# Laying the gate and silu tiles at the end of SBUF, and normalising row tile 1 before the statistics of row tile 2

## The chip, the cores and the metric

The kernel runs on one core of a Trainium2 chip. The metric is the device time of one execution in microseconds (us), as a median over several runs. A profile records one execution, and its span runs from the first to the last recorded instruction.

## The reference

The computation takes 2048 rows `x` of width 640, normalises them, and runs an attention block and a feed-forward block on the same normalised rows. The feed-forward result, passed through silu, gates the attention result, and `x` is added back.

```python
def reference(A_x, A_k_cache, A_v_cache, A_wq, A_wo, B_x, B_w_gate, B_w_up, B_w_down):
    def _A_ref(x, k_cache, v_cache, wq, wo):
        ...                                    # 32 heads of width 192, the last 512 keys alone
        scores = jnp.einsum("bhqd,bhkd->bhqk", q, k) * (Dh ** -0.5)
        p = _softmax(scores, axis=-1)
        o = jnp.einsum("bhqk,bhkd->bhqd", p, v)
        return (lambda x, *d: x.transpose(*d))(o, 0, 2, 1, 3).reshape(B, Sq, Hq * Dh) @ wo
    def _B_ref(x, w_gate, w_up, w_down):       # 640 -> 1536 -> 640
        g = _silu(x @ w_gate)
        u = x @ w_up
        return (g * u) @ w_down
    x = A_x
    xn = _layernorm(x, axis=-1)
    s = _A_ref(xn, A_k_cache, A_v_cache, A_wq, A_wo)
    g = _silu(_B_ref(xn, B_w_gate, B_w_up, B_w_down))
    return x + s * g
```

## The kernel before

Every engine executes its instructions in the order in which the program writes them; the order is written out by hand, and no scheduler changes it. There are three stages. The first normalises the rows and computes the feed-forward block. It leaves the transposed normalised rows in SBUF (`xnT`) and the gates in DRAM (`g_d`, 160 KB for each of 16 row tiles, stored on the SP queue by line 467 from the tiles `g_t`). The second computes the attention, two heads (a pair) at a time, in phases whose order is a table of tokens. The third multiplies by `wo`, applies the gates and stores the output.

**The opening.** The rows come in 16 row tiles of 128 rows; four of them make a block of 512. The first block is handled row tile by row tile. For row tile t, VectorE (DVE) takes two `bn_stats` over half rows (line 336) and a `bn_aggr` (line 339); ScalarE (ACT) takes the square root (line 368); DVE inverts it (line 377) and writes the normalised rows `xn` (line 379); TensorE (PE) transposes them with five matmuls against the identity (line 565); ACT copies the result into `xnT` in two parts (line 573). `ln_stats(t, between)` calls `between` after its first `bn_stats`. `ready(t)` issues the transposes and the copies, with the square root of row tile t + 1 between the two copies for t of 1 and 2.

```python
ln_stats(0)
ln_sqrt(0)
ln_stats(1, lambda: ln_apply(0, (slice(0, 2 * P), slice(2 * P, D))))
ready(0)
ln_sqrt(1)
...
for t in range(4):
    ...
    for k, (f, s, cs) in enumerate(order):
        if k == len(order) * 7 // 10 and t < 3:
            ...                                # the lines that the diff changes
            ready(t + 1)
        hidden_mm(first[f][s][:, rows], s, f, rows, cs)
```

`hidden_mm` (line 394) is one matmul, or five of them, of the gate or up projection, into six PSUM banks. So the transposes of row tile t + 1 stand in PE's order after 21 of the 30 matmuls of row tile t; for t = 0 the nine that follow read the late part of the up weights, `wu_sb`. The rows and the first weights are loaded on the SP and ACT queues in the order x tile 0, x tile 1, first weights, x tile 2, x tile 3, the other weights.

**The first stage's tiles.** Its pools are stacked from the end of SBUF downwards, in the order in which they are opened: `ffw` (weights, one scratch tile), `lnw` and `lnx` (statistics, `x_t` and `xn`), `ffh` (two hidden tiles `hT`), `ffa` (three `sg` tiles, which hold silu of the gate projection, and two `g_t` tiles). When the stage ends, all are closed, and the pools of the later stages take their bytes: `out_first` (operands of the third stage) from the end of SBUF downwards, then `m_f`, the two value tiles `V_p`, and `att_p` (nine `p_t` tiles for the exponentials of the scores). The first writer of a new tile waits for the last users of what lay there; in `att_p` the first tile waits for all users of the whole pool's bytes.

**The turn into attention.** The last gates are computed by ACT (line 464) and stored (line 467). The first phase then runs: scores (line 786, into two `sc` buffers of PSUM), exponentials on ACT (`p_t`, line 790), the queries in three forms (lines 717 and 729, added up by DVE in line 722 or by ACT, GpSimd and DVE with `m_f` in lines 747, 764, 767, 771 and 777), and probabilities times values (line 825). SP loads the values and transposes the keys of the next pair by DMA (`KT`, line 219). DVE sums those keys (line 227) and centres them (lines 236 and 238). In DVE's order the three key sums stand after the third line 722, and ahead of the first line 767, which PE needs before the next line 729 into the same bank.

Of the kernel before, what the change touches and what calls it, by code (L numbers as in the profile page):

```python
# [15 lines left out]
def kernel(  # L16
# [241 lines left out]
    a_q, b_w = {}, {}  # L258

    with ExitStack() as fctx:  # L260
        ffw = fctx.enter_context(tc.tile_pool(name="ffw", bufs=1, side="right"))
        lnw = fctx.enter_context(tc.tile_pool(name="lnw", bufs=4, side="right"))
        lnx = fctx.enter_context(tc.tile_pool(name="lnx", bufs=8, side="right"))
        ffh = fctx.enter_context(tc.tile_pool(name="ffh", bufs=2, side="right"))
        ffa = fctx.enter_context(tc.tile_pool(name="ffa", bufs=3, side="right"))

        zero_t = q_all[:, 0, :]
        nc.vector.memset(zero_t, 0.0)
# [61 lines left out]
        def ln_stats(t, between=None):  # L330
            b, ti = divmod(t, 4)
            if ti == 0:
                ln[b] = [lnw.tile([P, 4, 2], f32, name="mv"), lnw.tile([P, 4], f32, name="rstd")]
            stats = lnw.tile([P, ng, nc.vector.BN_STATS_DIM], f32, name="stats")
            for g in range(ng):
                nc.vector.bn_stats(stats[:, g, :], x_t[t][:, g * (D // ng) : (g + 1) * (D // ng)])
                if g == 0 and between:
                    between()
            nc.vector.bn_aggr(ln[b][0][:, ti, :], stats[:])
# [32 lines left out]
        def ln_apply(t, parts=(slice(0, D),)):  # L372
            b, ti = divmod(t, 4)
            mv, rstd = ln[b]
            xns[t] = lnx.tile([P, D], bf, name="xn", bufs=4)
            if b == 0:
                nc.vector.reciprocal(rstd[:, t : t + 1], rstd[:, t : t + 1])
            for cols in parts:
                nc.vector.tensor_scalar(
                    xns[t][:, cols], x_t[t][:, cols], mv[:, ti, 0:1] if b < 2 else mv[:, ti : ti + 1],  # L380
                    rstd[:, ti : ti + 1], op0=ALU.subtract if b < 2 else ALU.add, op1=ALU.mult,
                )
# [8 lines left out]
        def hidden_mm(out, s, f, qc, cs=range(NC)):  # L391
            w_sb = (wg_sb, wu_sb)[s]
            for c in cs:
                nc.tensor.matmul(  # L394
                    out, w_sb[:, c, f * P : (f + 1) * P], xnT[:, c, qc],
                    start=(c == 0), stop=(c == NC - 1),
                )

        def hidden_gate(b, f, g, u):
            sg = ffa.tile([P, 512], bf, name="sg")  # L400
            nc.scalar.activation(sg[:], g, ACT.Silu)  # L401
            nc.vector.tensor_tensor(hTs[b][:, f, :], u, sg[:], ALU.mult)  # L402
# [157 lines left out]
        def ready(t):  # L560

            xn, rows = xns.pop(t), slice(t * P, (t + 1) * P)
            for tp, cs in zip(tps, PARTS):
                for k, c in enumerate(range(cs.start, cs.stop)):
                    nc.tensor.transpose(tp[:, k, :], xn[:, c * P : (c + 1) * P], ident[:])
            for tp, cs in zip(tps, PARTS):
                part = tp[:, 0 : cs.stop - cs.start, :]
                if cs.stop == NC and 1 <= t < 3:
                    ln_sqrt(t + 1)
                if t == 3 and cs.stop == NC:  # L570
                    nc.vector.tensor_copy(out=xnT[:, cs, rows], in_=part)
                else:
                    nc.scalar.copy(xnT[:, cs, rows], part)
# [7 lines left out]
        for t in range(4):  # L581
            rows = slice(t * P, (t + 1) * P)

            order = [(*fs, [c]) for c in range(NC) for fs in banks]
            if t == 0:
                order = order[:12] + [
                    (f, s, [c]) for s in range(2) for c in range(2, NC) for f in range(3)
                ]
            elif t == 3:
                order = [(*fs, range(NC)) for fs in banks]  # L590
            for k, (f, s, cs) in enumerate(order):
                if k == len(order) * 7 // 10 and t < 3:
                    if t < 2:
                        ln_stats(t + 2, lambda: ln_apply(t + 1))
                    else:
                        ln_apply(t + 1)
                    ready(t + 1)
                    if t == 2:
                        nc.scalar.activation(act_t[:], one_t[:], ACT.Silu)
                hidden_mm(first[f][s][:, rows], s, f, rows, cs)  # L600
                if t == 3 and s == 1:
                    hidden_gate(0, f, *first[f])
# [573 lines left out]
    for s in range(PHASES_N):  # L1176
        table = FIRST if s < 4 else LAST if s >= PHASES_N - 4 else PHASES
        for x in table[s % 4].split():
            name = x.lstrip("+<")
# [55 lines left out]
```

## Time and profile before

| | |
|---|---|
| Median of three runs | 873.0 us (871.72 to 877.42) |
| The profiled execution: its time | 872.65 us |
| Its span | 870.8 us |
| PE busy | 860.6 us (99% of the span) |
| DVE, ACT, GpSimd busy | 588.4, 450.4, 165.9 us |
| Clock granted to TensorE | 1.0 of full speed |

A busy share is an average over the span. The profile's view of waits says who waited for whom, its timeline gives each engine's instructions in order, its chain of waits follows the end of the program back to what released each step, and a view of stretches gives busy times between two points of the span. Start times are in us from the start of the span.

### The profile page before, as it was taken

Reading aid. Unit: us, or ns where it says so; the run is one execution under the profiler, and the core shown is the slowest. Engines: PE = TensorE matmul, PEld = TensorE weight load, DVE = VectorE, ACT = ScalarE, POOL = GpSimd, SP = SyncE. Lnnn points to the kernel's source line nnn. Section 1 sums busy time; section 2 is a strip of 40 time slices with the busy share of each in tenths; the row PEclk is TensorE's granted clock in tenths of the full one; section 3 lists DMA queues with packets and bytes.
Section 4 is the critical chain, followed back from the end, with each engine's and each line's share of the span. In section 5 each row is a group of like instructions: output and inputs, shape, how many; then the busy total and the mean of one; then the engine's idle time right before and its main releaser. Section 6 shows DMA issues by size and latency. Waiting matters only on the chain.

```text
span 870.8 us, 22711 instructions
## 1 busy us (share of the span) xinstructions
PE 860.6 (99%) x9619; PEld 571.6 (66%) x9635; DVE 588.4 (68%) x1023; ACT 450.4 (52%) x634; POOL 165.9 (19%) x247
## 2 busy tenths in 40 slices
PE   8999999999999999999999999999999999999998
PEld 5455555567666666666666666666676777777776
DVE  6643666777777777777777777777755786655564
ACT  4264434567777677667667667667668400000000
POOL 0000000013224333333333333333331000000000
PEclk9999999999999999999999999999999999999999
DMA  9424423457789988988988967788898986655410
GB/s 298 95 46 112 84 72 84 96 99 135 179 162 161 186 179 176 229 178 180 232 173 191 224 147 175 173 184 163 191 223 197 268 283 223 211 178 174 176 54 16
DMA packets 264678, 143.87 MB, mean 165 GB/s; under 512 B 173696, under 2 KB 260480, under 8 KB 264576
## 3 DMA queue, kind: packets, MB, share of 16 engines
q1 hardware_dynamic: 263792, 141.77, 70.1%
q8 instruction: 75, 1.23, 0.6%
q10 hardware_dynamic: 784, 0.65, 0.2%
q14 instruction: 27, 0.22, 0.1%
HBM read 76.58 MB, written 30.41 MB: 123 GB/s over the span
## 4 chain that ended last, share of the span: by engine, by line
PE 96%; DMA 2%; ACT 1%; issue 0%; DVE 0%; ACTq 0%; POOL 0%; POOLq 0%; SPq 0%
PE acc L943 21%; PE sc L786 19%; PE mm L825 14%; PE mm L729 12%; PE sc L394 11%; PE sc L729 7%; PE mm L455 5%; PE sc L825 5%; PE mm L717 1%; PE sc L522 1%; DMA x_t<-in_A_x_dram 1%; ACT p_t L790 0%; PE gu L394 0%; DMA o_d<-OT_b 0%; DMA g_d<-g_t 0%
## 5 line engine op out<-in xcount | busy, mean ns | idle before, releaser
L790 ACT ACTIVATE p_t<-sc 128x1024 bf16<-128x1024 f32 x256 | 258.3, 1023 | 88.9 <-PE sc L786 86.1
L786 PE MATMUL sc<-q_all,khat 64*128 64x512 bf16 x1536 | 206.5, 376 | 2.3 <-ACT p_t L790 1.7
L825 PEld LDWEIGHTS <-p_t 64*128 64x128 bf16 x4096 | 179.7, 94 | 36.8 <-issue 0.6
L825 PE MATMUL mm<-V_p,p_t 64*128 64x193 bf16 x3008 | 157.3, 243 | 0.5 <-ACT O_b L854 0.3
L729 PEld LDWEIGHTS <-w_all 64*128 64x128 f16 (+1 forms) x1540 | 86.0, 94 | 71.4 <-issue 0.6
L786 PEld LDWEIGHTS <-khat 64*128 64x128 bf16 x1536 | 82.6, 94 | 58.4 <-issue 8.2
L771 POOL TENSOR_TENSOR m_f<-m_f 128x1024 f32<-128x1024 f32 x44 | 105.3, 2394 | 41.1 <-DVE r L843 15.0
L729 PE MATMUL mm<-xc,w_all 64*128 64x512 f16 x890 | 112.0, 376 | 0.0
L767 DVE TENSOR_TENSOR q_all<-mm,m_f 128x1024 bf16<-128x1024 f32 x44 | 53.9, 1224 | 56.2 <-ACT m_f L764 56.1
L943 PE MATMUL acc<-b_w,a_q 128*128 128x320 bf16 (+1 forms) x576 | 81.8, 299 | 0.0
L848 DVE TENSOR_TENSOR O_b<-mm,r 128x384 bf16<-128x384 f32 x151 | 78.3, 553 | 3.1
L993 ACT COPY xc<-acc 128x320 f32<-128x320 f32 x8 | 3.4, 426 | 135.7 <-PE acc L943 135.7
L802 POOL MEMSET turn_t<- 128x1 f32 x128 | 12.7, 99 | 314.8 <-PE mm L825 239.6
L943 PEld LDWEIGHTS <-a_q 128*128 128x128 bf16 x576 | 56.3, 98 | 22.0 <-issue 0.2
L402 DVE TENSOR_TENSOR hT<-sc,sg 128x512 bf16<-128x512 f32 x46 | 31.7, 691 | 55.2 <-ACT sg L401 55.2
L943 PEld LDWEIGHTS <-q_all 128*128 128x128 f16 x552 | 52.7, 98 | 19.1
L401 ACT ACTIVATE sg<-sc 128x512 bf16<-128x512 f32 x46 | 27.3, 596 | 67.7 <-PE sc L394 65.9
L777 DVE TENSOR_TENSOR q_all<-mm,m_f 128x1024 bf16<-128x1024 f32 x44 | 53.7, 1219 | 11.6 <-POOL m_f L771 7.8
L394 PE MATMUL sc<-xnT,wg_sb 128*128 128x512 bf16 (+1 forms) x247 | 59.5, 353 | 0.8
L394 PE MATMUL sc<-xnT,wu_sb 128*128 128x512 bf16 (+1 forms) x260 | 60.3, 354 | 0.0
L943 PE MATMUL acc<-b_w,q_all 128*128 128x320 f16 (+2 forms) x432 | 58.1, 292 | 0.0
L825 PE MATMUL sc<-V_p,p_t 64*128 64x193 bf16 x1088 | 53.7, 243 | 0.3 <-POOL turn_t L802 0.3
(125 smaller groups left out, 958.8 us busy)
## 6 DMA issues: line engine op xcount, KB each, us to landing
o_d<-OT_b SPq DMA_DIRECT2D x64, 384.0 KB, 4.1
a_q<-o_d SPq DMA_DIRECT2D x32, 768.0 KB, 6.3
wq_rows<-in_A_wq_dram SPq DMA_DIRECT2D x16, 480.0 KB, 4.6
wq_rows<-in_A_wq_dram SPq DMA_DIRECT2D x30, 240.0 KB, 5.5
K_p<-in_A_k_cache_dram SPq DMA_DIRECT2D x32, 192.0 KB, 3.4
V_p<-in_A_v_cache_dram SPq DMA_DIRECT2D x32, 192.0 KB, 4.2
b_w<-in_A_wo_dram SPq DMA_DIRECT2D x12, 480.0 KB, 4.4
g_d<-g_t SPq DMA_DIRECT2D x16, 160.0 KB, 1.8
```

The lines of the kernel that those rows point to most:

```text
L394: nc.tensor.matmul(out, w_sb[:, c, f * P : (f + 1) * P], xnT[:, c, qc], start=(c == 0), stop=(c == NC - 1),)
L402: nc.vector.tensor_tensor(hTs[b][:, f, :], u, sg[:], ALU.mult)
L455: nc.tensor.matmul(ps, left[:, c, :], D_OF[m][:, c, :], start=(first and c == 0), stop=(c == KD - 1), skip_group_check=True,)
L729: nc.tensor.matmul(ps[:, h, :], ws[h][r, c, :], xs[h][r, c, :], start=(first and c == 0), stop=(c == NC - 1), skip_group_check=True,)
L767: nc.vector.tensor_tensor(to[:, 1:3, :], st["ps"][:, :, :], m_f[:, 5:3:-1, :], ALU.add)
L771: nc.gpsimd.tensor_tensor(SIDE, diag, SIDE, ALU.subtract)
L777: nc.vector.tensor_tensor(to[:, 0:4:3, :], st["ps"][:, :, :], SIDE, ALU.add)
L786: nc.tensor.matmul(sc[:, h, :], khat[r, j, ks], q_of(i, j)[r, :], start=(j == 0), stop=(j == 2))
L790: nc.scalar.activation(p_t[:, :, :], sc[:, :, :], ACT.Exp, scale=scale)
L825: m = nc.tensor.matmul(acc[:, k, h * 256 : h * 256 + Dh + 1], Ps[i][kc][r, h, qt * P : (qt + 1) * P], V_of[i // NB % 2][r, kc, h, 0 : Dh + 1],
L848: nc.vector.tensor_tensor(O_b[:, qt, :, :], a_k[:, :, 0:Dh], r[:, k, :, :].to_broadcast([P, 2, Dh]), ALU.mult,)
L943: nc.tensor.matmul(ps[:, 0:w], at[:, c, :], b_w[m][:, c, k * w : (k + 1) * w], start=(first and c == 0), stop=(c == KH - 1), skip_group_ch ...
```

## The change

The pool `ffa` is opened first of the five, not last. So the `sg` and `g_t` tiles take the last 5632 bytes of each SBUF partition, and every other tile of the first stage's pools moves 5632 bytes down; nothing else moves. In the opening, for t = 0 alone, the normalisation of row tile 1 is written ahead of both `bn_stats` of row tile 2, where before it stood between them. Lines after 593 have numbers higher by 3 in the changed kernel.

```diff
     with ExitStack() as fctx:
+        ffa = fctx.enter_context(tc.tile_pool(name="ffa", bufs=3, side="right"))
         ffw = fctx.enter_context(tc.tile_pool(name="ffw", bufs=1, side="right"))
         lnw = fctx.enter_context(tc.tile_pool(name="lnw", bufs=4, side="right"))
         lnx = fctx.enter_context(tc.tile_pool(name="lnx", bufs=8, side="right"))
         ffh = fctx.enter_context(tc.tile_pool(name="ffh", bufs=2, side="right"))
-        ffa = fctx.enter_context(tc.tile_pool(name="ffa", bufs=3, side="right"))
...
                 if k == len(order) * 7 // 10 and t < 3:
-                    if t < 2:
+                    if t == 0:
+                        ln_apply(t + 1)
+                        ln_stats(t + 2)
+                    elif t == 1:
                         ln_stats(t + 2, lambda: ln_apply(t + 1))
                     else:
                         ln_apply(t + 1)
```

The bytes of an SBUF partition that matter, before and after:

| tile | before | after | tiles of the later stages over the old bytes |
|---|---|---|---|
| `sg`, `g_t` | 134368 to 140000 | 223712 to 229344 | `p_t` (133856 to 152288) |
| `hT` (two) | 140000 to 164576 | 134368 to 158944 | `p_t`, `V_p`, `m_f` |
| `x_t` | 164576 to 174816 | 158944 to 169184 | `m_f` (158688 to 170976), `out_first` |
| `xn` | 174816 to 179936 | 169184 to 174304 | `out_first` (170976 to 229344) |
| weights, `s_sum` | 180448 to 229344 | 174816 to 223712 | `out_first` |

## The prediction

> **What bounds the kernel now.** First the page.
>
> ```profile
> span 870.8 us, 22711 instructions
> PE 860.6 (99%) x9619; PEld 571.6 (66%) x9635; DVE 588.4 (68%) x1023; ACT 450.4 (52%) x634; POOL 165.9 (19%) x247
> ```
>
> PE is the bound, and is without work for 870.8 - 860.6 = 10.2 us, 1.2% of the span. Nothing here removes PE work, so a gain is a part of these 10.2 us. The view of PE's waits names two places that the diff touches (total, times, longest):
>
> ```profile
> PE sc L786 <- ACT p_t L790: 1.7, 1, 1.7
> PE tp L565 <- DVE xn L379: 1.6, 2, 0.9
> ```
>
> The first lies at the turn into attention. The chain of waits of that stretch (start, length, what):
>
> ```profile
> 165.54 3.17 DMA g_d<-g_t
> 168.72 0.02 issue
> 168.74 0.04 ACTq L790
> 168.78 0.05 issue
> 168.82 1.03 ACT p_t L790
> 169.85 0.04 issue
> 169.90 0.82 PE sc L786 x6
> ```
>
> The first exponential waits until the last gate store has landed, since `p_t` lies where `g_t` lay. ACT's timeline has it idle for 1.79 us before 168.82; PE, with both `sc` buffers full, waits 1.72 us for the exponential's end.
>
> The second place is the opening, in the timeline (start, length, engine, line, what, idle before):
>
> ```profile
> 6.33 0.21 DVE L339 BATCH_NORM_AGGREGATE mv<-stats 128x2 f32<-128x12 f32 x1
> 7.58 0.49 DVE L336 BATCH_NORM_STATS2 stats<-x_t 128x6 f32<-128x320 bf16 x1 [1.05 <-DMA x_t<-in_A_x_dram]
> 7.99 0.15 DVE L377 RECIPROCAL rstd<-rstd 128x1 f32<-128x1 f32 x1
> 8.18 0.45 DVE L379 TENSOR_SCALAR xn<-x_t,mv,rstd 128x640 bf16<-128x640 bf16 x1
> 8.54 0.49 DVE L336 BATCH_NORM_STATS2 stats<-x_t 128x6 f32<-128x320 bf16 x1
> 9.06 0.21 DVE L339 BATCH_NORM_AGGREGATE mv<-stats 128x2 f32<-128x12 f32 x1
> ```
>
> DVE stands 1.05 us at the first statistics of row tile 2, whose load lands at 7.56. Queued behind are the inverse root and the normalisation of row tile 1, which need nothing of it: their root was there at 7.00 (ACT line 368, 6.70 + 0.30). PE's transposes come at 8.68; its last matmul before began at 7.58. The stretch 7.6 to 8.7 has PE busy for 0.16 of 1.10 us.
>
> **The opening, step by step.** No instruction is added or removed; a group of two moves ahead of one. Inverse root 7.03 (as the first row tile's, 5.05, stands 0.03 behind its root), normalisation 7.22 to 7.67, transposes at 7.72, 0.96 earlier. Then three things cut the 0.96.
> - The nine matmuls that follow need the late part of `wu_sb`: issued at 2.75, to landing 5.4, so 8.15. They start at 8.17 instead of 8.97: 0.80 left.
> - What is pushed back: the statistics of row tile 2. They follow the normalisation at 7.58 and 8.03 (the pitch of the pair at 3.56 is 0.45), aggregate 8.48 to 8.69. That is earlier than 9.27, as the second statistics no longer stand behind line 379.
> - Their root sits on ACT between the two copies of row tile 1, so the second copy waits for it. Before: root 9.30, copy 9.50 to 9.96, and PE reached the matmuls that need it at 10.14 without waiting. Now root 8.72, copy 8.92 to 9.38, matmuls at 9.40; PE would be ready at 8.17 + 21 x 0.0556 = 9.34. So 10.14 - 9.40 = 0.74 is left.
>
> Row tiles 2 and 3 follow: x tile 3 lands at 3.28 + 5.4 = 8.68, where DVE wants it at 8.70; `xn` of tile 2 is then ready at 9.8 and PE wants it at 9.9. The next weights land at 12.0, long ahead of use. From 15 to 165 us PE is busy for 149.16 of 150, so an earlier start reaches the turn. Bounds: 0 (a landing jitter eats it) to 0.96; I take 0.74.
>
> **The turn.** The bytes of `p_t` now lie where only `hT` lay, whose readers are done by 164. In the instruction order of the changed program the first exponential waits for PE alone. What takes over: the `m_f` copy on ACT (line 747) gets two waits on DMAs, those that loaded or transposed row tiles; the last of these (line 385) was issued at 100.9, so it costs nothing at 171. Times below are those of before, without the 0.74.
> - The exponential follows the table load and its small activation, 167.03 to 168.05. PE's 20 matmuls of line 717 from 165.84 last until 168.0. Scores at 168.11 instead of 169.90: 1.79.
> - The third line 717 needs the bank that the first sum of line 722 frees (167.74 to 168.96, behind 3.54 us of weight sums): 169.0 instead of 170.54, so 1.54 is left.
> - Then DVE is late:
>
> ```profile
> 167.74 2.35 DVE L722 TENSOR_REDUCE q_all<-mm 128x512 bf16<-128x1024 f32 x2
> 171.84 1.22 DVE L722 TENSOR_REDUCE q_all<-mm 128x512 bf16<-128x1024 f32 x1 [1.75 <-PE mm L717]
> 173.09 1.87 DVE L227 TENSOR_REDUCE ssum<-KT 128x1 f32<-128x512 bf16 x3
> 175.21 0.71 DVE L238 TENSOR_SCALAR khat<-KT,nmean 64x512 bf16<-64x512 bf16 x2
> 176.12 1.23 DVE L767 TENSOR_TENSOR q_all<-mm,m_f 128x1024 bf16<-128x1024 f32 x1 [0.20 <-ACT m_f L764]
> ```
>
> The third sum now ends at 171.5, and DVE comes to the key sums. Their `KT` is a DMA issued at 167.91 behind the store and two value loads on SP, which move with nothing here; to landing 5.0, so 172.91. Before, DVE came at 173.09 and the landing was hidden; now DVE stands 1.4 us. The key sums move by only 0.14, line 767 (its 0.20 of idle gone as well) to 175.80 and its end to 177.03. Behind it on PE:
>
> ```profile
> 177.23 0.83 PE L786 MATMUL sc<-q_all,khat 64*128 64x512 bf16 x6
> 177.88 1.26 PE L729 MATMUL mm<-xc,w_all 64*128 64x512 f16 x10
> ```
>
> Line 729 adds into the bank that line 767 reads: 177.09 instead of 177.88. So 0.79 stays of 1.54, and 0.75 comes back as a new wait on DVE. After it the bank of line 825 is free at 178.25 for a start at 178.82, and that of the next line 717 at 181.6 for 182.13. From 180 to 684 PE is busy for 502.66 of 504 us, nothing to give or take. Bounds: 0 to 1.72.
>
> **The sum.** -0.74 - 0.79 = -1.53 us: span 870.8 to 869.3, the profiled execution 872.65 to 871.1. That execution lies 0.35 under the median; on the median, 873.0 - 1.5 = 871.5.
>
> **Rivals.**
> - Whole gain at the turn: `KT` lands early (its 16 landings are 3.7 to 5.0, median 3.9) or line 767 doesn't hold PE. At 3.9 it lands at 171.8, the key sums move by 1.1 and the turn gives 1.5: -2.3, 870.7. Against it: this is the slowest landing of the 16, with two value loads beside it, which are still there.
> - `KT` lands later still: 1.3 later (the spread of its own landings) turns 0.79 into -0.51; the sum is -0.2, 872.8.
> - The change does half of what it says: another wait holds the first exponential, or x tile 3 or the weights hold PE in the opening. One place alone: -0.75, 872.2.
> - Slower: the operands of the first stage run worse at their new bytes; hidden tiles and weights all move by 5632. The place is the 150 us from 15 to 165, the price 1.5 us for each per cent, so it decides from 1% on (ten matmuls of line 394 in 2.18 us, not 2.16). At 2%: -1.5 + 3.0, 874.5; a loss of over 1% needs 7%. For it: no row shows these bytes. Against: gate and up weights, 15360 bytes apart, have means of 353 and 354 ns.
>
> The Trainium skill, page "SBUF — State Buffer", section "SBUF: two separate sides", says that among the engines only the port shared by VectorE and GpSimd makes one wait for another, and that TensorE and ScalarE never wait there. By that rule the slower rival costs nothing; the two means agree as far as they go, and no run here shows the new bytes.
>
> **How the numbers follow.** Forecast 0.57, whole gain 0.12, half 0.10, `KT` later 0.09, new bytes 0.08; the 0.04 left is for a gain beyond these, out of phases that fall otherwise from 165 us on. 1% is 8.7 us, about what a measurement of this kernel can tell from no change. No case gives that much faster (it would take nearly all of PE's 10.2 us), so it has the 0.04 left over. Of the new bytes I give 0.04 to a loss over 1%. Within 1%: 0.92. The lower end is the whole gain less the run-to-run step from the median of before to its fastest run (1.28): 870.7 - 1.3 = 869.4. The upper end is 874.5, the 2% case, which also holds an unchanged 873.0 with the same step of 1.3 the other way (the runs reach 877.42).
>
> **What would show it.** Right: transposes of row tile 1 near 7.7 and PE's first-stage work earlier by 0.7; the first exponential straight behind the small activation; the key sums with an idle of over 1 us put down to `KT`; line 729 of 177.88 waiting for line 767. Wrong: an exponential that still waits for a DMA, key sums that move as far as the exponential, line 394's pitch changed, or a PE total that is not 860.6.

## The result, and the profile after

The median fell from 872.91 to 870.86 us (20 runs of each, 871.72 to 877.42 and 870.38 to 872.13), a ratio of 0.9971 [0.9963, 0.998]. The profiled execution took 870.84 us (before: 872.65), its span is 1.8 us shorter, and the page begins:

```profile
span 869.0 us, 22724 instructions
PE 862.4 (99%) x9635; PEld 572.3 (66%) x9635; DVE 588.3 (68%) x1023; ACT 450.8 (52%) x634; POOL 165.8 (19%) x247
```

PE's total rose from 860.6 to 862.4, but the trace of before lacks 16 matmul records (9619 beside 9635 weight loads), so the two totals can't be subtracted. The matching of weight load to weight load, 9635 in each trace, can: it says how much earlier each instruction of PE starts. That is 0.58 us at 10 us, the same until the turn, 2.11 behind the turn, 1.77 at 232 us, 1.83 at the end. So 0.58 came in the opening, 1.53 at the turn, and 0.3 was lost at 231 us.

The view of PE's waits (total, times, longest) in the changed kernel:

```profile
PE gu L323 <- DVE q_all L268: 1.2, 1, 1.2
PE mm L828 <- ACT O_b L857: 0.6, 1, 0.6
```

Both waits of the prediction are gone: that of the scores for the first `p_t` (1.7 before) and that of the transposes for `xn` (1.6 in two). What stands at the head now is the wait ahead of the first matmul of all, and 0.6 at one line 828 at 230 us, which was 0.31 before: there the keys of another pair landed late and DVE stood 0.91 us for them, which is the 0.3 lost.

The opening in the timeline (start, length, engine, line, what, idle before):

```profile
7.13 0.16 DVE L377 RECIPROCAL rstd<-rstd 128x1 f32<-128x1 f32 x1 [0.72 <-ACT rstd L368]
7.33 0.45 DVE L379 TENSOR_SCALAR xn<-x_t,mv,rstd 128x640 bf16<-128x640 bf16 x1
7.70 0.88 DVE L336 BATCH_NORM_STATS2 stats<-x_t 128x6 f32<-128x320 bf16 x2
7.84 0.45 PE L565 MATMUL tp<-ident,xn 128*128 128x128 bf16 x5
```

The normalisation of row tile 1 stands ahead of the pair of statistics, and the transposes follow it at 7.84, where before they came at 8.68. The turn, in the same view:

```profile
166.24 0.20 ACT L692 ACTIVATE act_t<-one_t 128x1 f32<-128x1 f32 x1
166.35 2.95 ACT L793 ACTIVATE p_t<-sc 128x1024 bf16<-128x1024 f32 x3
167.41 0.83 PE L789 MATMUL sc<-q_all,khat 64*128 64x512 bf16 x6
...
169.72 1.23 DVE L725 TENSOR_REDUCE q_all<-mm 128x512 bf16<-128x1024 f32 x1 [0.22 <-PE mm L720]
171.12 1.87 DVE L227 TENSOR_REDUCE ssum<-KT 128x1 f32<-128x512 bf16 x3 [0.17 <-DMA KT<-K_p]
...
174.00 1.23 DVE L770 TENSOR_TENSOR q_all<-mm,m_f 128x1024 bf16<-128x1024 f32 x1
175.76 1.26 PE L732 MATMUL mm<-xc,w_all 64*128 64x512 f16 x10
```

The first exponential follows the small activation with no wait for the store, and the scores behind it start with no idle time ahead. The third sum of line 725 ends at 170.95 and the key sums start at 171.12: they wait 0.17 us for `KT`, not the 1.4 that the prediction gave. Its DMA was issued at 167.10 and landed 4.0 us later, where in the profile of before it took 5.0. Counted with the 0.58 us of the opening, the scores moved by 2.5 us, the key sums by 2.0, and line 732 (177.88 before, now 175.76) by 2.1.

### The profile page after: what moved, and what is told of

The parts are those of the page before. It is cut to its first block, busy times and chain, and to the rows that moved or that the text cites. A ratio compares the mean times of both kernels' runs of the same rounds, so it can differ in the third digit from the quotient of the medians.

```text
span 869.0 us, 22724 instructions
## 1 busy us (share of the span) xinstructions
PE 862.4 (99%) x9635; PEld 572.3 (66%) x9635; DVE 588.3 (68%) x1023; ACT 450.8 (52%) x634; POOL 165.8 (19%) x247
## 4 chain that ended last, share of the span: by engine, by line
PE 96%; DMA 1%; DVE 1%; ACT 1%; issue 0%; SPq 0%; POOL 0%; ACTq 0%; POOLq 0%
PE acc L946 21%; PE sc L789 18%; PE mm L828 14%; PE sc L394 11%; PE mm L732 11%; PE sc L732 7%; PE mm L455 5%; PE sc L828 5%; PE mm L720 1%; DMA KT<-K_p 1%; PE sc L522 1%; PE gu L323 1%; PE gu L394 1%; DMA o_d<-OT_b 0%; DVE w_all L173 0%; DMA OT_b<-O_b 0%
```

## The experiments

Three things were open. Is the gain the layout's, the order's, or both? Does the give-back through `KT` that the prediction counted exist at all? And is the opening's 0.58 the work of the change? The theory was that both parts gain, the layout at the turn and the order in the opening; its rivals were that one part alone does it, and that the key landing, not the removed store wait, sets what the turn gives. All runs below had five rounds against the kernel before on the same chip; the ratio is that to the kernel before.

| run | what it is | median (range), us | ratio |
|---|---|---|---|
| e1 | layout alone | 872.73 (870.53 to 875.12) | 0.9986 [0.9972, 1.0] |
| e2 | order alone | 873.74 (871.94 to 876.44) | 0.9998 [0.9984, 1.0011] |
| e3 | change, `KT` issued later | 878.46 (876.81 to 880.26) | 1.0051 [1.0031, 1.007] |
| e4 | change, `KT` issued earlier | 872.27 (870.33 to 874.85) | 0.9978 [0.9963, 0.9993] |
| f1 | change again | 872.13 (870.88 to 874.07) | 0.9973 [0.9961, 0.9985] |
| f2 | change, key centrings moved | 870.78 (870.56 to 871.4) | 0.996 [0.9945, 0.9974] |
| f3 | before, key centrings moved | 873.23 (872.79 to 874.62) | 0.9989 [0.9976, 1.0002] |
| f4 | f2 and `KT` earlier | 870.79 (870.37 to 871.01) | 0.9957 [0.9941, 0.9973] |
| g0 | before, centrings moved | 873.09 (872.22 to 875.35) | 1.0001 [0.9991, 1.0012] |
| g1 | layout alone, centrings moved | 871.57 (870.41 to 873.43) | 0.9978 [0.9969, 0.9986] |
| g2 | order alone, centrings moved | 874.14 (872.05 to 875.53) | 1.0002 [0.9994, 1.0011] |
| g3 | change, centrings moved | 871.1 (870.59 to 871.36) | 0.9968 [0.9957, 0.998] |

Runs e1 to e4 shared one chip, f1 to f4 a second, g0 to g3 a third; the kernel before had medians of 874.5, 874.33 and 873.28 there.

### e1 and e2: each part alone

The edit

```diff
+        ffa = fctx.enter_context(tc.tile_pool(name="ffa", bufs=3, side="right"))
         ffw = fctx.enter_context(tc.tile_pool(name="ffw", bufs=1, side="right"))
...
-        ffa = fctx.enter_context(tc.tile_pool(name="ffa", bufs=3, side="right"))
```

is e1, with the opening as before, and e2 has the pools as before and

```diff
-                    if t < 2:
+                    if t == 0:
+                        ln_apply(t + 1)
+                        ln_stats(t + 2)
+                    elif t == 1:
```

> The pool of gates and silu tiles opened first, the opening left as it was. Theory of two gains: the first exponential follows the table load, PE's 1.7 us wait at the turn is gone, PE reaches the turn no earlier than in the kernel before, and the time is about 1.5 us under before if the key transpose lands 4.0 us after its issue, about 0.8 us if it lands after 5.0. Rival (the layout pays everything and the opening nothing): about 2.0 us under before, as the whole change. Rival (new bytes slow the first stage): ten matmuls of line 394 take more than 2.16 us.

> Row tile 1 normalised ahead of the statistics of row tile 2, the pools as they were. Theory of two gains: transposes of row tile 1 near 7.7 to 7.9 us, not 8.7; PE's work is earlier by 0.6 to 0.75 us from 10 us on, keeps that up to the turn, still waits 1.7 us there for the exponential behind the gate store, and the time is 0.6 to 0.75 us under before. Rival (the layout pays everything): the time is that of before, within 0.2 us, since the lead is lost on the way to the turn.

The order alone gave nothing that can be measured, so its forecast missed, and the time is the one that the rival gave. The layout alone had a median 1.8 us under before, near its forecast of 1.5, but with an interval that touches 1. Both profiles held something that no theory had named.

In e2, as in the kernel before, the first exponential waits for the last gate store, now for longer, as the store landed after 3.73 us and not 3.17: PE stands 2.27 us. What follows is slow. The view of stretches of e2 (from and to, us of stretch; then for PE, weight loads, DVE, ACT, GpSimd the busy time and instructions; then granted clock, and DMA):

```profile
168.00:170.50 2.50, 0.41 (x4) 0.16 (x5) 1.73 (x2) 1.49 (x2) 0.00 (x0) 0.88 1.11 156
170.50:173.50 3.00, 3.00 (x18) 1.30 (x16) 0.00 (x0) 1.47 (x2) 0.00 (x0) 0.53 1.00 265
173.50:176.00 2.50, 2.50 (x27) 1.22 (x24) 2.35 (x3) 1.01 (x1) 0.00 (x0) 1.00 1.12 222
```

In the 3 us behind the idle time the granted clock was 0.53, then 1.00 again: 3 x 0.47, so some 1.4 us lost by this estimate, and the mean clock of the whole run reads 0.998.

In e1 the rows at 543 us show the second thing:

```profile
544.43 2.54 DVE L238 TENSOR_SCALAR khat<-KT,nmean 64x512 bf16<-64x512 bf16 x1
544.48 2.35 POOL L771 TENSOR_TENSOR m_f<-m_f 128x1024 f32<-128x1024 f32 x1 [0.39 <-DVE q_all L767]
...
548.30 1.47 PE L786 MATMUL sc<-q_all,khat 64*128 64x512 bf16 x12 [1.37 <-DVE O_b L848]
```

The same place in the kernel before:

```profile
545.48 0.35 DVE L238 TENSOR_SCALAR khat<-KT,nmean 64x512 bf16<-64x512 bf16 x1
545.53 2.51 POOL L771 TENSOR_TENSOR m_f<-m_f 128x1024 f32<-128x1024 f32 x1 [0.39 <-DVE q_all L767]
```

The two starts lie 0.05 us apart in both kernels; in e1 the key centring lasts as long as GpSimd's whole operation, 2.54 us instead of 0.35, DVE is late, and PE waits 1.37 us. The instructions and their order are the same: it is a race that comes out either way. Line 238 took 2.54 us once in the profiles of e1, e2 and f1 and twice in e3 and e4, and never in those of before and after. No profile of the kernel before itself shows it, but e2, with the old layout, does; so it is tied to neither the layout nor the order, and it blurs small differences.

### e3 and e4: the key transpose moved on SP's queue

Both are the change with one token of the first phase's table moved: `ktO`, which issues the key transposes, is put behind the load of the next weights (e3) or ahead of the value loads (e4).

```diff
-        "wcO0 wcO1 s0 s1 +TT11 wpO vlE TT00 ktO wlE ah s2 TT11 ksO0 DGsa RD RS1 s3 ksO1 ksO2 kcO0 s4 klE kcO1 "
+        "wcO0 wcO1 s0 s1 +TT11 wpO vlE TT00 wlE ktO ah s2 TT11 ksO0 DGsa RD RS1 s3 ksO1 ksO2 kcO0 s4 klE kcO1 "
```

and, for e4, of the same line

```diff
+        "wcO0 wcO1 s0 s1 +TT11 wpO ktO vlE TT00 wlE ah s2 TT11 ksO0 DGsa RD RS1 s3 ksO1 ksO2 kcO0 s4 klE kcO1 "
```

> The whole change, with the DMA transpose of the second pair's keys issued behind the three query-weight loads on SP, not ahead of them: its issue moves by about 1.9 us. Theory (the key sums stand in front of line 770 on DVE, and PE needs line 770): the key sums move by 1.9 to 2.9 us, line 732 behind the scores at 175.1 by 1.4 to 2.4 us, and the time is 1.4 to 2.4 us over that of the whole change, so between 0.6 under and 0.4 over before. Rival (the landing is hidden): the time of the whole change, within 0.2 us.

> The whole change, with the same DMA transpose issued ahead of the two value loads on SP: its issue moves 1.7 us earlier, the value loads land about 2 us later, still 2 us or more ahead of their use. Theory: with a landing after 4.0 us the key sums of the whole change stand only 0.17 us, so the time is that of the whole change to 0.2 us less; where some executions of the whole change have a landing of 5.0 us, the median gains up to 0.5 us more. Rival (the landing doesn't matter): no difference at all from the whole change, and the key sums show no idle either way.

In e3 the transposes were issued at 169.68 and landed after 6.2 us. Its timeline:

```profile
175.88 1.87 DVE L227 TENSOR_REDUCE ssum<-KT 128x1 f32<-128x512 bf16 x3 [4.94 <-DMA KT<-K_p]
...
180.01 2.31 PE L732 MATMUL mm<-xc,w_all 64*128 64x512 f16 x10 [4.07 <-DVE q_all L770]
```

The chain that the prediction wrote down (key landing, key sums, line 767 of before, line 729 of before) is there with all its links. PE stood 4.07 us for it, and the ten matmuls behind took 2.31 us instead of 1.26, again at half the clock. So e3 lost more than the late landing by itself: the forecast of 1.4 to 2.4 us over the change was too low. Against e4, the nearest kernel on that chip, the median was 6.2 us higher. The landing came 4.8 us later than in after (175.88 for 171.12), as both the issue and the time to landing moved, and the half clock came on top. In e4 the key sums no longer waited, but two key centrings took 2.54 us beside GpSimd, and the time is not told apart from that of the change (0.9978 and, in f1, 0.9973).

### f1 to f4: the raced key centrings moved

Of the key centrings, one stood right behind line 767, whose end also starts GpSimd's line 771. Now both stand ahead of line 767, in the table of the phase in question; six other key centrings of each execution, in another phase, still start 0.05 us ahead of line 771.

```diff
-        "s0 <1b0.s RS1 <1b1a <kcE3 RA <1a0.s <kcE4 <0b0.1 <1a1v <0b1v RB s1 RM ktO <sp1 s2 <<sp1 wcO1 s3 +klE "
+        "s0 <1b0.s RS1 <kcE3 <kcE4 <1b1a RA <1a0.s <0b0.1 <1a1v <0b1v RB s1 RM ktO <sp1 s2 <<sp1 wcO1 s3 +klE "
```

f2 is the change with this edit, f3 the kernel before with it, f4 is f2 with the edit of e4, and f1 the change alone once more.

> The changed kernel itself, once more, beside the kernel before and next to the runs below. In the profiles of the first four runs the key centring of line 238 that follows line 767 on DVE starts 0.05 us ahead of GpSimd's line 771 and then takes 2.54 us, not 0.35, in some executions; PE then waits 1.4 us. Theory of the lock: the runs of this kernel fall into steps of about 1.8 us above the fastest, whose number differs from execution to execution. Theory of two gains: its median is 1.3 to 2.6 us under that of the kernel before on this chip. Rival (what the change gains is chance of the first comparison): the median is within 0.5 us of that of before.

> The whole change, and in the repeated phases the last two key centrings (line 238) put ahead of the division that DVE waits for, so that none follows line 770 directly. Theory of the lock: no line 238 of 2.5 us is left, the runs lose their steps of 1.8 us, and the median is 0.5 to 2 us under that of the changed kernel, its fastest run within 0.3 us of the fastest there. Rival (the 2.5 us come from something else, such as the late key transpose): line 238 still has values of 2.5 us and the spread of the runs is as before.

> The kernel before with the same two key centrings moved, the change not made. Theory: the steps of 1.8 us from line 238 go, but PE's wait at the turn stays, and with it a second step: where that wait is over about 2 us, PE's clock is granted at 0.50 for some 3 us behind it, and the run has a mean clock of 0.998 and is about 1.6 us longer. So the median is 0.5 to 2 us under before, and runs of clock 0.998 are still there. Rival (the slower runs of before all come from line 238): no run with 0.998 is left and the spread is that of the changed kernel with the same move.

> The whole change, the moved key centrings, and the key transpose of the second pair issued ahead of the value loads. Theory: the transpose lands before DVE comes to its key sums in every execution, so the last source of spread at the turn is gone: a median 0 to 0.5 us under that of the change with the moved centrings alone, and 2.5 to 4 us under before. Rival (the landing at the turn no longer matters once the exponential is free): equal to it within 0.2 us.

No profile of a kernel with the moved centrings (f2 to f4, g0 to g3) has a line 238 above 1.59 us. The seven other profiles hold 42 meetings at the place that was emptied, six in each, and all seven cases of 2.54 us are among them. At the six places that stayed, the key centring was short in all 84 meetings of the 14 profiles, though the starts are as close. GpSimd had ended a small instruction 0.39 us before the meetings of the first kind, and 0.8 us or more before those of the second; whether that decides was not tested. The change with them ran at 870.78 and 870.79, with a spread of 0.8 and 0.6 us where f1 spread over 3.2. These are the best versions of the study. Moving `KT` as well adds nothing that can be measured, and the intervals of f1, f2 and f4 overlap, so that the centrings make the change faster is likely from the spread and not shown by the ratios. f1 lay 2.2 us under before on its chip, as forecast. f3 lay 1.1 us under it, and 3 of its 12 runs still had a mean clock of 0.998, so the raced centrings were not the only source of slower runs of before.

The profile of f3, which has the opening of before, shows what that opening does in another execution:

```profile
7.07 0.49 DVE L336 BATCH_NORM_STATS2 stats<-x_t 128x6 f32<-128x320 bf16 x1 [0.68 <-DMA x_t<-in_A_x_dram]
7.30 0.28 PE L394 MATMUL sc<-xnT,wg_sb 128*128 128x128 bf16 x2 [0.19 <-DMA wg_sb<-in_B_w_gate_dram]
...
8.16 0.45 PE L565 MATMUL tp<-ident,xn 128*128 128x128 bf16 x5 [0.19 <-DVE xn L379]
```

With nothing changed in the opening the transposes wait 0.19 us, not 0.94, and PE has waited for the late gate weights before.

### g0 to g3: each part alone, without the race

> The kernel before with the two key centrings moved, as in an earlier run; it is the base for the three runs below, which have the same move, so that the steps from line 238 are in none of them. Expected as before: 872.8 to 873.3 us at a mean clock of 1.0, and some runs of clock 0.998 about 1.5 us higher.

> The layout alone, with the moved key centrings. Theory (the turn gives its whole 1.5 us, and keeps PE's clock): 1.5 to 1.9 us under the base, no run of clock 0.998. Rival (the layout pays all of the change): 2.3 us or more under the base, equal to the whole change.

> The new order alone, with the moved key centrings. Theory (an earlier PE only waits longer for the landing of the last gate store, which is bound to the ScalarE chain behind the last gates and moves with PE): 0.3 to 0.6 us under the base. Rival (the lead is swallowed, since a longer wait drops the clock more often): the time of the base or over it, with more runs of clock 0.998.

> The whole change with the moved key centrings. Theory (the parts add): 1.8 to 2.5 us under the base, 0.3 to 0.6 us under the layout alone. Rival (the opening adds nothing): equal to the layout alone within 0.2 us.

The edits are those of e1 and e2 and the change itself, each with the centrings moved as in f3 (g0 is f3 and g3 is f2, on another chip). Now the four cases stand apart: the order alone 1.0002 [0.9994, 1.0011], the layout alone 0.9978 [0.9969, 0.9986], both 0.9968 [0.9957, 0.998]. The layout carries the change: PE's wait for the first `p_t` is in all five profiles with the old layout (1.72 to 2.38 us) and in none of the nine with the new one. What the order adds to it is 0.47 us in the medians of g1 and g3, with intervals that overlap; that it adds anything is not shown. g2 missed its forecast: its median lay 1.05 us over g0's, with a mean clock of 0.998 in 6 of 12 runs, where g0 had 5. That fits the rival as to the time, but 6 against 5 does not show that the order makes the drop more frequent. g1 met its forecast (1.52 under g0), but for one run of 0.998.

g1 also shows the forecast give-back. Its `KT` was issued at 167.82, as late as before, and took 4.2 us:

```profile
172.00 1.87 DVE L227 TENSOR_REDUCE ssum<-KT 128x1 f32<-128x512 bf16 x3 [1.10 <-DMA KT<-K_p]
...
176.13 1.26 PE L729 MATMUL mm<-xc,w_all 64*128 64x512 f16 x10 [0.23 <-DVE q_all L767]
```

DVE stands 1.10 us, and PE's line 729 comes 0.42 us later against the start of its turn than in after (10.92 us behind its first line 717, after 10.50). In g3 the idle time of DVE was 0.85 and line 732 came 0.18 later, in e1 0.72 and 0.04 (line 729); in f2 (0.53), f1 (0.45) and after (0.17) nothing came back. So DVE could stand some 0.68 us before PE felt it.

## Why the prediction was right, and where its terms were wrong

The sum of the prediction was -1.53 us, the span fell by 1.8 and the median by 2.05. Its two terms were both mis-sized, with opposite signs, so it is luck that the total came so near.

**The opening: -0.74 forecast, -0.58 in one pair of profiles, nothing to -0.2 in the mean.** In the two profiles that were compared the steps look right: normalisation 7.33 (7.22 forecast), transposes 7.84 (7.72). PE's last matmul ahead of the transposes of before began at 7.52, not at 7.58 as the prediction has it, which changes no term. But the 14 profiles of this study hold 5 with the opening of before and 9 with the new one. PE's matmuls that need the second copy of row tile 1 start at 10.14, 9.63, 9.78, 10.28 and 9.52 in the first group, a mean of 9.87; and from 9.56 to 10.44 in the second, a mean of 9.86. With single profiles some 0.3 us off their mean, so few can't exclude a small gain. What mostly holds PE there is the landing of the late gate weights, ahead of the transposes: in 11 of the 14 profiles it stands 0.18 to 1.00 us for them. Its first matmul on these weights starts between 7.1 and 8.4 us, and in every profile but one the second-copy matmuls come 2.0 to 2.3 us behind that, with either opening. The one is the profile of before: PE found these weights there at 7.07, the earliest of all, x tile 2 came late (7.56), and the gap was 3.07. Measured from these weights, then, the old opening costs 0.2 us in the mean (2.32 against 2.10), nearly all of it from that one profile. The transposes waited for `xn` in two of the five profiles with the old opening, 0.94 us in before and 0.19 in f3. The step that failed is the one that took the 0.96 us from a single execution and chose 0.74 between the bounds of 0 and 0.96. The "half" rival had the reason (the weights hold PE in the opening), with 0.10. Nor does the wait for the store swallow a lead: in all five profiles with that wait the store is issued 0.30 us ahead of PE's first line 717 or 720, and PE's wait is the store's time to landing less some 1.46 us.

**The turn: -0.79 forecast, -1.53 measured.** The removed wait and its first two steps came out as written. The exponential follows the small activation, and without the opening's 0.58 the scores moved by 1.91 (1.79 forecast); behind line 722's bank 1.53 was left (1.54). The step that failed is the last, "KT landing 5.0": it landed after 4.0, 3.9, 4.8, 4.0, 4.2 and 4.1 us in after, f1, f2, e1, g1 and g3, and in after it was issued 0.81 earlier than in before, 0.58 of it the opening's. Beyond the opening's 0.58 the key sums therefore moved by 1.39, not by 0.14, and line 767 did not hold PE. That is the rival "whole gain at the turn" as to the cause. Its own total, 870.7, lies nearer to 870.86 than the forecast does. Against it stood that the two value loads beside `KT` were still there; they were, and it landed earlier all the same. The change is not the reason: with the old layout the same DMA took 5.0 us in before and e2, 4.7 in g2, 3.9 in f3 and 3.8 in g0. So 5.0 was one of the values that this landing takes, and which one comes these runs do not explain. The chain behind the landing was right: with DVE idle for 1.4 us, the 0.68 us that DVE could stand leave 0.72 for PE, and the prediction had 0.75.

**What the prediction left out.** The size of the removed wait itself varies. In the chain of waits the last store landed after 3.17 us in the profile of before, the least of five: 3.48, 3.56, 3.73 and 3.84 in g0, g2, e2 and f3. PE's wait at the turn went from 1.7 to 2.4 us with it, and the layout's gain there, taken from after against g0 and f3, was 1.84 and 2.20. In two of the five profiles with that wait, e2 and g2, the clock then fell to half. Mean clocks of 0.998 or less stood in 34 of 132 runs of the kernels that have the wait, and in 2 of 88 of those with the new layout (without e3, which has another long wait). Such runs are longer: for the kernel before, 875.06 against 873.08 in the medians of one chip. So a quarter of the executions pay some 2 us more, about 0.5 us in the mean, and the layout takes that away. The narrower spread of after fits this, though the runs do not show that nothing else is in it.

**The other points.** Line 394 kept its pitch (ten matmuls in 2.16 us), so the slower rival of the new bytes fell. "`KT` later still" did not come, but e3 shows that its price would have been above what the prediction gave, since a wait of PE of 4 us costs clock besides. PE's total could not be used as a test, because of the missing records. That the change stays within 1% came out: no cause found here is near 8.7 us.

## What to carry to other kernels

A tile that is laid over a buffer whose store is still in flight inherits the landing of that store; put buffers with late DMAs where the next stage writes last. Read a DMA landing from several executions before a term of a sum rests on it: here one profile made an opening of 0.96 us out of what is nothing to 0.2 us in the mean. When a trace shows an instruction that takes seven times as long in some executions, as here the key centring beside the subtraction on GpSimd, look for what starts within 0.1 us of it on another engine, and order one of them away from the other.

## What the runs showed of the hardware

**The clock falls after a short idle time, and the position of that time decides.** The granted clock in the six profiles with a PE wait of over 1.7 us:

| run | PE idle, us | longest part inside one stretch of 3.41 us | granted clock behind it |
|---|---|---|---|
| before | 1.72 | 1.72 | 1.00 |
| g0 | 2.02 | 1.10 | 1.00 |
| f3 | 2.38 | 2.06 | 1.00 |
| g2 | 2.10 | 2.10 | 0.50 from 171.88 to 175.29 |
| e2 | 2.27 | 2.11 | 0.50 from 169.92 to 173.33 |
| e3 | 4.07 | 2.69 | 0.50 from 178.63 to 185.46 |

The half clock lasted 3.41 us, 3.41 us and twice that. It began a whole number of times 3.413 us after the first full clock that its trace records: 48 times in e2 (from 6.08 us on), 49 in g2 (from 4.62) and 51 in e3 (from 4.55). The third column lays the same grid over every profile (from 3.97 us on in before, 5.07 in g0, 4.15 in f3). So the clock fell where 2.10 us or more of one stretch were idle, and not at 2.06 or less; f3's longer wait lay across a border. The grid and the limit are inferred from these six profiles alone. The Trainium skill, page "TensorE: Matmul & The Clock Gate", section "What's actually happening", describes a free-running window of about 3.4 us and half the clock after an idle one. The window and the half clock agree; but here a window that was idle for 2.10 of its 3.41 us was enough.

**VectorE and GpSimd, all or nothing.** A `tensor_scalar` of 64x512 bf16 on DVE that starts 0.05 us ahead of GpSimd's `tensor_tensor` took 0.35 or 2.54 us in the 126 meetings of the 14 profiles, with nothing between. GpSimd's took 2.50 to 2.52 us where DVE's was short, and 2.35 in the seven meetings where it was long. The Trainium skill, page "SBUF — State Buffer", section "Who interferes with whom", has the two engines locking each other out of a shared port for certain operations; the 2.54 us agree with a lock held for the whole of GpSimd's instruction. It gives the lock to whoever issues first; in the trace of e1 DVE's instruction starts 0.05 us ahead and still waits, so the starts in the trace don't say who wins.

**A DMA's landing differs from execution to execution.** The same key transposes at the same place of SP's order landed after 3.8 to 5.0 us, with either layout, and after 6.2 in the one profile in which they were issued behind one load more; the last gate store landed after 3.17 to 3.84 us.
